# Gated linear attention and a feed-forward block on one core: scores computed over all 128 queries and masked 512 columns at a time, from the ninth chunk on

## The chip, the cores and the metric

The kernel runs on one NeuronCore of a Trainium2 chip. The metric is the device time of one execution in microseconds (us), given as the median of several runs. Beside the timed runs there is one profiled execution, from which all the views of the profile are read.

## What is computed

The reference has two stages. The first is a gated recurrence over 768 steps, for 4 batches and 8 heads of 48 values each. The second is a feed-forward block on the 3072 resulting rows of 384 values.

```python
for t in range(S):                                   # S = 768, D = 48
    state = alpha[:, :, t, :, None] * state + einsum('bhd,bhe->bhde', k[:, :, t], v[:, :, t])
    y[:, :, t] = einsum('bhd,bhde->bhe', q[:, :, t], state)
x = y.transpose(0, 2, 1, 3).reshape(B * S, H * D)    # 3072 x 384
a = x @ w1
b = x @ w2
out = ((a * b) @ w3) @ w_out
```

## The kernel before

The recurrence is done in chunks of 128 steps: 24 chunks (4 batches of 6), numbered n = 0 to 23, of all 8 heads at once. For a chunk, the products of the gates become a prefix sum of logarithms (`logs`, `decays`), its exponential scales k and q (`decayed`, DVE, L354), and 16 TensorE transposes with two ScalarE copies (`transposed`, L376 and L378) put k and q with their 48 values on the partitions (`qkT`). The heads stand in pairs: head 2j (called i = 0) on partitions 0 to 47, head 2j+1 (i = 1) on partitions 64 to 111, for j = 0 to 3. Then

- `scores(n)`: for each head, keys times queries, a 128 x 128 block. The blocks of the four heads of one i fill one bank of PSUM, `sc[i]`, of 512 columns. Scores of a key that is later than the query have to become zero, so VectorE writes `ms`, the scores and-ed bit by bit with a mask of all ones and zeros (L452, or L435).
- `attend_state(n-1)` (L469) brings in what earlier chunks left in the state; `attend(n-1)` (L477, L480) multiplies the values with the masked scores of the chunk before, and ScalarE copies the result out (L484).
- `outer(n)` (L388) and `advance(n)` carry the state on.

Up to chunk 7 a head's scores are one matmul over the whole width of the array (L449), and a mask is one instruction of 512 columns per i (L452). From chunk 8 on (`TURNED = 8`), `turned_scores` uses the array as four quarters of 64 x 64. The row half of a quarter is given by i, its column half by where the output lies: for i = 0, keys 0 to 63 (part 0) go to partitions 0 to 63 of the bank and keys 64 to 127 (part 1) to partitions 64 to 127; for i = 1 the two halves are exchanged ("turned"), so that the four matmuls of one j lie in four different quarters. Keys of part 1 are later than queries 0 to 63, so their matmul covers only the 64 queries 64 to 127; a part 0 matmul covers all 128. The 64 x 64 block that is left out is neither computed nor masked, and no one reads it: `attend_low` (L414) multiplies queries 0 to 63 with keys 0 to 63 alone, over half the rows of the array, and `attend` (L477) does queries 64 to 127 with all 128 keys. Two `attend_low` matmuls of the chunk before follow the four score matmuls of each j. For i = 1 the values, too, are needed with their halves exchanged: `turn_v` (GpSimd, L166) makes that copy.

Because of the block left out, the masks are four instructions per chunk (L435): for each i one of 64 partitions x 256 columns (queries 0 to 63; for i = 1 it begins at partition 64) and one of 128 x 256.

Beside the chunks, the same loop converts the weights of the feed-forward block from 64-bit words (`to_fp32`, L238 to L248, then L255 to L260), stores the attention's output to memory (L300), reads it back in groups of three chunks (`load_x`, L496), splits it into three parts (`split_x`, L502 on ScalarE, L503 and L504 on VectorE), and already runs `early_gate`, the products with w1 and w2 (L510), whose results ScalarE (L519) and VectorE (L521, L558) take out of PSUM. After the chunks come the rest of these products and the fold of w3 with w_out, and at last the product with the folded weights; all three run L510.

What sets the order: each engine works through its own queue in order[...]. The queue's order isn't that of the source; a scheduler lays it out when the program is built, by its own estimate of what each instruction takes, within the limits that the kernel gives with `tc.issue_after`. The same scheduler chooses for each of the 430 tiles taken with `bank()` one of the 8 banks of PSUM. A matmul that starts a tile waits until the tile that had this bank before has been read.

Of the kernel before, what the change touches and what calls it, by code (L numbers as in the profile page):

```python
# [12 lines left out]
I32 = mybir.dt.int32  # L13
# [3 lines left out]
ALU = mybir.AluOpType  # L17
# [31 lines left out]
def kernel(  # L49
# [12 lines left out]
    nc = tc.nc  # L62
    B, H, S, D = q.shape
    C = 128
# [4 lines left out]
    NP = H // 2  # L69
    DP = 64  # L70
# [34 lines left out]
    def bank():  # L105
        return ps.tile([C, 512], FP32, tag="bank", name="bank")
# [53 lines left out]
    def turned(n):  # L160
        return TURNED <= n < N
# [30 lines left out]
    keep = p1.tile([C, C], I32, name="keep")  # L192
    keep_turned = p1.tile([C, 2, DP], I32, name="keep_turned")
# [12 lines left out]
    keep_bc = keep[:, None, :].to_broadcast([C, NP, C])  # L206
    for half in range(2):
        nc.gpsimd.tensor_copy(out=keep_turned[ds(DP * half, DP), 1 - half], in_=keep[ds(DP * half, DP), ds(DP * half, DP)])
    nc.gpsimd.memset(keep_turned[DP:, 1], -1)
    for x in qks:  # L210
        nc.vector.memset(x[:, :, :, D:], 0.0)
    make_identity(nc, ident)
# [197 lines left out]
    def attend_low(n, jj, i, half):  # L410

        s, w = ds(DP * i, DP), (vts[n % 2] if i else st["v", n])
        h = half * NP // 2 + jj
        nc.tensor.matmul(st["y", n][0][i][ds(DP * half, DP), jj, 0:DP], w[s, h if i else 2 * h, :],  # L414
                         st["ms", n][s, i, h, 0:DP], start=(n % NCH == 0 and jj == 0), stop=True, skip_group_check=True)

    def turned_scores(n):

        qkT = st["qkT", n]
        sc = [bank().rearrange("p (j c) -> p j c", j=NP) for _ in range(2)]  # L420
        for j in range(NP):
            for part in range(2):
                for i in range(2):
                    r, t = ds(DP * i, D), slice(DP * part, C)
                    nc.tensor.matmul(sc[i][ds(DP * (part ^ i), DP), j, t], qkT[r, 0, j, ds(DP * part, DP)],  # L425
                                     qkT[r, 1, j, t], start=True, stop=True)
            if turned(n - 1):
                for i in range(2):
                    attend_low(n - 1, j % 2, i, i ^ (j < 2))
        ms = work.tile([C, 2, NP, C], FP32, tag="ms", name="ms")  # L430
        for i in range(2):
            r = ds(DP * i, DP)
            low, high = (keep_turned[r, 0], keep_turned[:, 1]) if i else (keep[r, 0:DP], keep[:, DP:])
            for x, mask, t in ((slice(DP * i, DP * (i + 1)), low, slice(0, DP)), (slice(0, C), high, slice(DP, C))):
                masked = nc.vector.tensor_tensor(ms[x, i, :, t].bitcast(I32), sc[i][x, :, t].bitcast(I32),  # L435
                                                 mask[:, None, :].to_broadcast([x.stop - x.start, NP, DP]),
                                                 op=ALU.bitwise_and)
        ends_of_part1[0] = mark["ms", n] = masked.ins
        st["ms", n] = ms

    def scores(n):
        if turned(n):
            return turned_scores(n)
        qkT = st["qkT", n]
        sc = [bank().rearrange("p (j c) -> p j c", j=NP) for _ in range(2)]
        for j in range(NP):
            for i in range(2):
                r = ds(DP * i, D)
                nc.tensor.matmul(sc[i][:, j, :], qkT[r, 0, j, :], qkT[r, 1, j, :], start=True, stop=True)  # L449
        ms = work.tile([C, 2, NP, C], FP32, tag="ms", name="ms")  # L450
        for i in range(2):
            masked = nc.vector.tensor_tensor(ms[:, i].bitcast(I32), sc[i].bitcast(I32), keep_bc, op=ALU.bitwise_and)  # L452
        ends_of_part1[0] = mark["ms", n] = masked.ins
        st["ms", n] = ms
# [345 lines left out]
    low, high = range(FH), range(FH, KF)  # L800
# [74 lines left out]
```

## Time and profile before

| | us |
|---|---|
| median of 3 runs | 471.29 |
| lowest and highest | 470.62, 471.86 |
| the profiled execution | 472.93 |
| its span in the trace | 471.20 |
| of the span: chunks 0 to 7, up to the first turned scores | 69.6 |
| of the span: turned chunks 8 to 23, and the last attend | 69.6 to 186 |
| of the span: rest of the feed-forward block | 186 to 471.2 |

The views of the profile give busy time by engine: PE is TensorE's matmuls, PEld its weight loads, DVE VectorE, ACT ScalarE, POOL GpSimd, SP the queue of most DMAs. An fp32 matmul appears as two records, one for each pass over its columns. The end of a matmul is modelled, so the distance from one start to the next says more than the length of a record. Every line of a list of waits names the instruction that waited, what it waited for, the total, the number of times and the longest.

### The profile page before, as it was taken

How to read it: one execution, taken by the hardware profiler on the slowest of the kernel's cores; microseconds unless marked ns; L12 is line 12 of the kernel's file. 1: busy time of each engine (PE TensorE's matmuls, PEld its weight loads, DVE VectorE, ACT ScalarE, POOL GpSimd, SP SyncE). 2: the span in 40 equal slices, each digit the busy share in tenths (PEclk: the TensorE clock that was granted, in tenths of full speed). 3: DMA queues.
4: the chain of work that ended last, by engine and by line, in shares of the span. 5: the costliest groups of instructions: out<-in, count | busy, mean ns of one | idle time of the engine just before them, and what ended most of it. 6: DMA issues, size and time to landing. Idle time of an engine off the chain costs nothing.

```text
span 471.2 us, 11168 instructions
## 1 busy us (share of the span) xinstructions
PE 453.1 (96%) x4360; PEld 430.4 (91%) x4360; DVE 363.5 (77%) x610; ACT 278.9 (59%) x552; POOL 96.0 (20%) x186
## 2 busy tenths in 40 slices
PE   4996999999999999999999999999999999999996
PEld 2675889898999989999999999999999999999996
DVE  2876997999979898999999968764542977766771
ACT  4864975767767554889787656554553633333330
POOL 6332243234313550222221111111011000000000
PEclk9999999999999999999999999999999999999999
DMA  9999999999999953566685433212013886555511
GB/s 182 251 189 247 239 226 207 222 218 207 203 207 209 266 141 116 170 185 220 205 297 190 133 124 101 85 50 85 35 51 111 245 243 184 176 160 167 173 52 50
DMA packets 145668, 80.36 MB, mean 171 GB/s; under 512 B 96240, under 2 KB 137456, under 8 KB 145616
## 3 DMA queue, kind: packets, MB, share of 16 engines
q1 hardware_dynamic: 139840, 64.44, 55.2%
q0 software_dynamic: 5776, 15.22, 10.3%
q8 instruction: 34, 0.56, 0.5%
q14 instruction: 18, 0.15, 0.1%
HBM read 57.58 MB, written 22.06 MB: 169 GB/s over the span
## 4 chain that ended last, share of the span: by engine, by line
PE 86%; DMA 5%; DVE 4%; ACT 3%; issue 1%; SPq 0%; DVEq 0%; ACTq 0%
PE bank L510 70%; DMA kq<-in_q_dram 3%; PE bank L425 3%; PE bank L376 2%; PE bank L477 2%; PE bank L469 2%; PE bank L612 1%; PE bank L388 1%; PE bank L338 1%; PE bank L341 1%; DMA raw<-in_moe_w_dram 1%; PE bank L480 1%; DVE qk L354 1%; PE bank L414 1%; PE bank L449 1%
## 5 line engine op out<-in xcount | busy, mean ns | idle before, releaser
L510 PE MATMUL bank<-x,w 128*128 128x384 f32 x1152 | 212.4, 338 | 1.9 <-DVE ms L435 0.9
L510 PEld LDWEIGHTS bank<-x,w 128*128 128x128 f32 x1152 | 199.9, 188 | 4.4 <-DVE ms L435 1.0
L510 PE MATMUL bank<-w3o,ab 128*128 128x384 f32 x576 | 100.2, 336 | 0.0
L510 PEld LDWEIGHTS bank<-w3o,ab 128*128 128x128 f32 x576 | 99.8, 188 | 0.0
L535 ACT ACTIVATE bank<-bank 128x384 f32<-128x384 f32 x96 | 45.6, 476 | 43.0 <-PE bank L510 42.8
L519 ACT ACTIVATE t<-bank 128x384 f32<-128x384 f32 x64 | 31.6, 495 | 54.8 <-PE bank L510 54.6
L585 POOL DMA_DIRECT2D abd<-ab x45 | 25.7, 570 | 143.4 <-DVE ab L571 126.8
L571 DVE TENSOR_TENSOR ab<-bank,r 128x384 f32<-128x384 f32 x44 | 24.4, 555 | 25.6 <-ACT bank L535 16.4
L378 ACT COPY qkT<-bank 128x512 f32<-128x512 f32 x48 | 26.0, 591 | 24.2 <-PE bank L376 24.2
L641 DVE TENSOR_TENSOR ab<-abl,ab 128x1024 fp32r<-128x1024 f32 x24 | 29.4, 1224 | 13.0 <-ACT ab L640 13.0
L640 ACT ACTIVATE ab<-abl 128x1024 fp32r<-128x1024 f32 x24 | 25.5, 1061 | 20.2 <-PE bank L510 18.0
L510 PE MATMUL bank<-wo,w3T 128*128 128x384 f32 x192 | 35.9, 334 | 0.0
L354 DVE TENSOR_TENSOR qk<-kq,e 128x768 f32<-128x768 f32 x24 | 23.3, 971 | 15.0 <-ACT e L345 7.5
L510 PEld LDWEIGHTS bank<-wo,w3T 128*128 128x128 f32 x192 | 33.5, 188 | 0.0
L243 ACT ACTIVATE power<-power,rebias 128x512 uint32<-128x512 uint32 (+1 forms) x36 | 25.1, 700 | 12.2 <-DVE power L242 12.1
L521 DVE SCALAR_TENSOR_TENSOR o<-bank,t 128x384 f32<-128x384 f32 x24 | 13.4, 557 | 22.4 <-issue 13.7
L642 DVE SCALAR_TENSOR_TENSOR ab<-ab,abl 128x1024 fp32r<-128x1024 f32 x24 | 29.2, 1219 | 0.0
L521 DVE SCALAR_TENSOR_TENSOR r<-bank,t 128x384 f32<-128x384 f32 x40 | 22.1, 552 | 6.8 <-ACT t L519 4.1
L245 DVE SCALAR_TENSOR_TENSOR mant<-mant,rest 128x512 f32<-128x512 uint32 (+1 forms) x36 | 23.6, 655 | 2.0 <-ACT rest L238 1.9
L238 ACT ACTIVATE rest<-raw 128x512 f32<-128x512 uint32 (+1 forms) x36 | 23.4, 652 | 1.0 <-DMA raw<-in_moe_w_dram 1.0
L166 POOL COPY vt<-v 64x192 f32<-64x192 f32 x32 | 19.4, 606 | 22.0 <-DMA v<-in_v_dram 21.0
L246 DVE SCALAR_TENSOR_TENSOR power<-raw,power 128x512 uint32<-128x512 uint32 (+1 forms) x36 | 23.3, 655 | 0.3 <-ACT power L243 0.2
(104 smaller groups left out, 685.9 us busy)
## 6 DMA issues: line engine op xcount, KB each, us to landing
raw<-in_moe_w_dram SPq DMA_DIRECT2D x28, 512.0 KB, 5.3
abl<-abd SPq DMA_DIRECT2D x24, 512.0 KB, 4.3
abd<-ab POOLq DMA_DIRECT2D x45, 192.0 KB, 3.1
xT<-xd POOLq DMA_DIRECT2D x9, 576.0 KB, 4.4
kq<-in_k_dram SPq DMA_DIRECT2D x24, 192.0 KB, 5.0
kq<-in_q_dram SPq DMA_DIRECT2D x24, 192.0 KB, 5.8
xd<-x SPq DMA_DIRECT2D x48, 96.0 KB, 3.9
out_dram<-o SPq DMA_DIRECT2D x24, 192.0 KB, 3.4
```

The source lines that it names most:

```text
L243: nc.scalar.activation(power, power, AF.Relu, scale=2.0 ** 23, bias=rebias)
L354: mark["qk", n] = nc.vector.tensor_mul(qks[n % 3][:, :, :, 0:D], st.pop(("kq", n)), st.pop(("e", n)).rearrange("p i (h d) -> p i h d", h=H ...
L378: mark["qkT", n] = nc.scalar.copy(qkT[:, :, :, ds(DP * half, DP)], tp[half]).ins
L510: nc.tensor.matmul(p, w[part][i], x[part][i], start=start and part == parts[0] and i == 0, stop=stop and part == parts[-1] and i == n - 1, ...
L519: nc.scalar.activation(t, p1, AF.Copy, scale=(1.0 + 1.0 / P) * scale)
L521: nc.vector.scalar_tensor_tensor(to, p2, scale, t, op0=ALU.mult, op1=ALU.add)
L535: nc.scalar.activation(p, p, AF.Copy, scale=1.0 + 1.0 / P)
L571: nc.vector.tensor_mul(ab, p, r[0])
L585: (nc.gpsimd if late else nc.sync).dma_start(out=abd[g][:, f, :], in_=ab)
L640: nc.scalar.activation(t[:, 0], ab, AF.Copy, scale=1.0 - 2.0 ** -13)
L641: nc.vector.tensor_sub(t[:, 1], ab, t[:, 0].bitcast(FP32))
L642: nc.vector.scalar_tensor_tensor(t[:, 2], t[:, 0].bitcast(FP32), -1.0 - 1.0 / P, ab, op0=ALU.mult, op1=ALU.add)
```

## The change

`turned_scores` now computes part 1, too, over all 128 queries; its 64 x 64 blocks that no one reads are computed and then masked to zero. That makes a mask one instruction of 128 partitions x 512 columns per i. For i = 1 the mask is the 128 x 128 tile `keep_turned`, read whole; its quarter that was never used (partitions 0 to 63, first 64 columns) is now set to 0 by one more memset in the setup. The `attend_low` matmuls stand in two groups of four, after j = 1 and after j = 3, one in each quarter of the array, instead of two after every j. The values stay in their two copies, and `attend`, `attend_low` and everything after the chunks are as they were. Line numbers in the text are those of the kernel before.

```diff
@@ setup
     nc.gpsimd.memset(keep_turned[DP:, 1], -1)
+    nc.gpsimd.memset(keep_turned[0:DP, 0], 0)
@@ turned_scores
         for j in range(NP):
             for part in range(2):
                 for i in range(2):
-                    r, t = ds(DP * i, D), slice(DP * part, C)
-                    nc.tensor.matmul(sc[i][ds(DP * (part ^ i), DP), j, t], qkT[r, 0, j, ds(DP * part, DP)],
-                                     qkT[r, 1, j, t], start=True, stop=True)
-            if turned(n - 1):
-                for i in range(2):
-                    attend_low(n - 1, j % 2, i, i ^ (j < 2))
+                    r = ds(DP * i, D)
+                    nc.tensor.matmul(sc[i][ds(DP * (part ^ i), DP), j, :], qkT[r, 0, j, ds(DP * part, DP)],
+                                     qkT[r, 1, j, :], start=True, stop=True)
+            if turned(n - 1) and j % 2:
+                for half in range(2):
+                    for i in range(2):
+                        attend_low(n - 1, j // 2, i, half)
         ms = work.tile([C, 2, NP, C], FP32, tag="ms", name="ms")
         for i in range(2):
-            r = ds(DP * i, DP)
-            low, high = (keep_turned[r, 0], keep_turned[:, 1]) if i else (keep[r, 0:DP], keep[:, DP:])
-            for x, mask, t in ((slice(DP * i, DP * (i + 1)), low, slice(0, DP)), (slice(0, C), high, slice(DP, C))):
-                masked = nc.vector.tensor_tensor(ms[x, i, :, t].bitcast(I32), sc[i][x, :, t].bitcast(I32),
-                                                 mask[:, None, :].to_broadcast([x.stop - x.start, NP, DP]),
-                                                 op=ALU.bitwise_and)
+            mask = keep_turned.rearrange("p x c -> p (x c)")[:, None, :].to_broadcast([C, NP, C]) if i else keep_bc
+            masked = nc.vector.tensor_tensor(ms[:, i].bitcast(I32), sc[i].bitcast(I32), mask, op=ALU.bitwise_and)
```

## The prediction

> **What bounds the kernel now.** I read first the busy times of the page, then the same by stretches of time, then who TensorE waited for while the turned chunks run, and last the order of time inside one score block.
>
> ```profile
> span 471.2 us, 11168 instructions
> PE 453.1 (96%) x4360; PEld 430.4 (91%) x4360; DVE 363.5 (77%) x610; ACT 278.9 (59%) x552; POOL 96.0 (20%) x186
> ```
>
> ```profile
> 68.00:92.00 24.00, 23.51 (x415) 21.50 (x417) 20.70 (x40) 16.44 (x38) 6.87 (x15) 1.00 0.94 208
> 92.00:116.00 24.00, 23.32 (x458) 21.17 (x451) 23.56 (x47) 16.36 (x37) 8.48 (x16) 1.00 0.98 215
> ...
> 186.00:300.00 114.00, 114.00 (x666) 113.87 (x667) 105.20 (x193) 88.21 (x176) 22.12 (x36) 1.00 0.53 173
> ```
>
> In the second fence the columns after the length are the busy times of PE, PEld, DVE, ACT and POOL. PE is the bound: over 23 of 24 us while these turned chunks run, all of the time from 186 to 300. DVE is close behind, 23.56 of 24 us from 92 to 116. So DVE's work matters only where PE waits for it:
>
> ```profile
> PE bank L510 <- DVE ms L435: 0.9, 2, 0.7
> PE bank L510 <- ACT qkT L378: 0.5, 1, 0.5
> PE bank L469 <- DVE ms L435: 0.3, 1, 0.3
> PE bank L425 <- ACT w L255: 0.2, 1, 0.2
> ```
>
> From 68 to 186 us the masks hold PE three times, for 1.2 us in all; these are matmuls that need a bank which the mask hasn't read yet. That is about what a faster mask can win directly. Now one score block, chunk 11:
>
> ```profile
> 91.32 0.67 PE L469 MATMUL bank<-qkT,T 48*64 48x128 f32 x16
> 91.81 0.38 PE L425 MATMUL bank<-qkT 48*64 48x128 f32 x7
> ...
> 92.80 0.22 PE L414 MATMUL bank<-ms,v 64*64 64x64 f32 x1
> ...
> 92.86 0.22 PE L414 MATMUL bank<-ms,v 64*64 64x64 f32 x1
> ...
> 93.03 0.71 PE L376 MATMUL bank<-ident,qk 64*128 64x64 f32 x16
> ```
>
> The block takes 1.22 us, from the first L425 to the first L376, and so in 11 of the 15 blocks with L414; the other four take 1.26.
>
> [...] the 16 passes of L469, 128 columns each over the four quarters, are through in 0.49 us (91.32 to 91.81), while on one quarter a pass follows the one before after 0.109 us. [...] at 172.5 (last fence) a copy stands behind an instruction that waits.
>
> **The change part by part.**
>
> *TensorE.* No instruction is added; per chunk the 8 part 1 matmuls grow from 64 to 128 columns. In the single starts of the trace a pass on one quarter takes 0.109 us for 128 columns and 0.058 for 64 (L414 above: 92.80, 92.86). Every matmul has two passes, and each quarter gets four score matmuls and two of L414. Before, the two quarters of part 0 had 4 x 2 x 0.109 + 2 x 2 x 0.058 = 1.10 us, the two of part 1 had 4 x 2 x 0.058 + 0.23 = 0.70. Afterwards all four have 1.10. The block lasts as long as its fullest quarter (1.10, and 0.12 until L376 begins, makes the 1.22 measured), so the added 0.40 us lies beside what the other two do: 0. The lower bound is -0.04 x 16 = -0.6 us, if the even grouping takes away the hiccup of the 1.26 blocks everywhere; the upper bound, no cover at all, is 16 x 0.40 = 6.4 us. I take 0, since L469 already shows four quarters at 128 columns each with no loss. Chunk 8, without L414, stays at 4 x 2 x 0.109.
>
> *VectorE.* Both shapes stand in the profile:
>
> ```profile
> L452 DVE TENSOR_TENSOR ms<-bank,keep 128x512 int32<-128x512 int32 x16 | 10.4, 683 | 0.0
> L435 DVE TENSOR_TENSOR ms<-bank,keep_turned 64x256 int32<-64x256 int32 x16 | 6.9, 428 | 0.5
> L435 DVE TENSOR_TENSOR ms<-bank,keep 128x256 int32<-128x256 int32 x16 | 6.5, 405 | 0.0
> ```
>
> Consecutive DVE instructions overlap, so I count from start to start. The four masks of a chunk take 0.334 + 0.437 + 0.442 + 0.342 = 1.555 us (chunk 11: starts at 95.39, 95.72, 96.16, 96.60 and the next instruction at 96.94)[...]. Two masks of 512 columns take 0.601 + 0.598 = 1.20 (chunks 0 to 7). DVE saves 0.355 us per chunk, 16 x 0.355 = 5.7 us. Since PE is the bound, nearly all of it becomes idle time of DVE. The memset in the setup, 0.15 us on POOL like its neighbour, lies between 1.8 and 3.7 us, when PE waits for the first gates: 0.
>
> *The order of the queues.* In the built programs PE's order is the same but for the L414. ACT, DVE, SP and POOL are laid out anew in places, and banks are assigned anew. Four places matter.
>
> 1. Chunk 6. Before, ACT puts one L484 copy (50.55) ahead of an L243 that waits for DVE until 51.80; now both copies stand behind it. The second, and all that follows, comes 0.25 us later. The third transposes after it need the first copy's bank, and the chain goes on to L502 and L273, for which PE stands still until 60.11: +0.25.
>
> 2. Chunk 11. PE waits 0.30 us at 96.0 for the first two masks, done at 96.13. Now an L239 and an L242 (0.33 + 0.34) stand ahead of the masks. Saved since 87 are 0.36 for chunk 10's masks and 0.06 on this one (0.68 instead of 0.74 until i = 0 is read): 0.67 - 0.36 - 0.06 = +0.25.
>
> 3. Chunk 13. L469 waits 0.45 us more than usual at 110.3 for the masks, the scores after it 0.39 for the last mask's bank (ended at 111.68; the profile names L255, which ends then too). Now the scores take a bank that was copied at 109.6, but the second half of L469 takes that of the turned mask, done at about 111.0 (masks begin 0.36 earlier and last 1.28). One stall of about 0.45 stays, the other goes: -0.3.
>
> 4. Chunk 22, the largest:
>
> ```profile
> 170.33 0.59 ACT L378 COPY qkT<-bank 128x512 f32<-128x512 f32 x1 [0.68 <-PE bank L376]
> 172.51 0.72 ACT L243 ACTIVATE power<-power,rebias 128x512 uint32<-128x512 uint32 x1 [1.60 <-DVE power L242]
> 173.15 0.56 ACT L378 COPY qkT<-bank 128x512 f32<-128x512 f32 x1
> ```
>
> One qkT copy stands ahead of L243, which waits for DVE, and one behind it. Now both stand behind. The bank of the first is the one for the L510 matmuls that start at 172.4; they wait until the copy ends, 173.15 + 0.56 = 173.71, and run 0.56 until 174.3. Before, the next group began at 173.80, after its own 0.88 us of waiting for a mask: +0.5.
>
> On SP the store of results, the loads of kq and the read-back L496 change places, but these loads run more than 10 us ahead (L496 issued at 150.54, used at 167.36): 0, and as much as they come late if that lead were used up.
>
> **The sum.** 0 + 0.25 + 0.25 - 0.3 + 0.5 = +0.7 us on the span of 471.2. The profiled execution itself took 472.93, 1.7 more than its span and 1.6 more than the median of the runs, so I carry the difference to the median: 471.29 + 0.7, forecast 472.0. About 0.3% (1.4 us) is what a measurement of this kernel can tell from no change; the forecast lies within it.
>
> **The rivals.**
>
> *The masks do win.* If the order moves cost nothing and all stalls that end with a mask go (0.30, 0.45, 0.39, 0.88), the time falls by 2.0 to 469.3. For it: three of them are named in the waits. Against: at 172 PE waits for L243 whatever the masks do, and all of PE's stalls from 68 to 186 are only some 3 us.
>
> *ACT's queue is the worse for it (slower).* The place is L243, which waits for DVE, ahead of copies that free banks. At chunk 22 its start follows L503, L504, L239 and L242 on DVE. If DVE reaches L242 there a microsecond later than at 172.5, PE stands still that microsecond more, since it has nothing else to run. Two such places with 0.8 us each and my +0.7 give 473.6. It decides from 0.7 us beyond what I reckoned. For it: the queues are laid out by estimates, and DVE's slow L242 (0.72 us in the record, 0.42 at most other places) beside two POOL copies shows that they needn't hold. Against: DVE has 0.73 us of idle time ahead of L503.
>
> *The columns aren't hidden.* If two quarters of the same rows share a limit that L469 doesn't show beside L414, the block grows by up to 0.40: 472.0 + 6.4 = 478.4.
>
> **How the numbers follow.** Forecast 66%, reaching from 470.3 to 472.7; masks win 7%; ACT's queue 21%, 472.7 to 474; columns not hidden 6%. The range goes from 470.3 to 474.0: it leaves out the unhidden columns, most of the win and a little of ACT's tail, about 15%. Faster by over 0.3% (below 469.9): 0.06. Slower (above 472.7): 0.21 + 0.06 = 0.27. Within: 0.67.
>
> **What would show it.** Score blocks from first L425 to first L376 still at 1.22; a block of 1.6 makes the third rival right. DVE's busy time about 5 to 7 us less (records, which overlap: for a chunk 1.665 now and 2 x 0.683 then, 16 x 0.30 = 4.8), the two masks 1.2 us from start to start. PE idle at 172.4 until about 173.7 on L378, and the first L510 of chunk 7 at about 60.4. If PE's stalls from 68 to 186 sum to under 1.5 us, my reckoning of the order is wrong; if PE stands still at places where it doesn't now, the second rival is at work.

## The result: 1.2% slower

| | before | after |
|---|---|---|
| median, us | 471.31 (6 runs) | 477.36 (6 runs) |
| ratio, 95% interval | | 1.012, 1.0086 to 1.0153 |
| the profiled execution, us | 472.93 | 477.86 |
| its span, us | 471.2 | 476.2 |
| of it, from the first score matmul of chunk 8 to the end, us | 401.7 | 408.2 |

The forecast of 472.0 and its range, up to 474.0, are both missed. Lines of the changed kernel stand one further than those of the kernel before up to the scores, and two earlier behind the masks: the wide scores are L426 (was L425), `attend_low` L415 (L414), the transposes L377 (L376), the qkT copies L379 (L378), the first feed-forward products L508 (L510). On POOL, `vt` stays L166, the decay products are L406 and L407 (L405, L406), the loads of the decays L363 (L362), the stores of end rows L327, L348 and L350 (L326, L347, L349).

### The profile page after: what moved, and what is told of

Read it like the earlier page. It is cut to its first block, busy times and chain, and to the rows that moved or that the text cites. A ratio compares the mean times of both kernels' runs of the same rounds, so it can differ in the third digit from the quotient of the medians.

```text
span 476.2 us, 11116 instructions
## 1 busy us (share of the span) xinstructions
PE 457.4 (96%) x4360; PEld 433.0 (91%) x4360; DVE 358.5 (75%) x578; ACT 279.1 (59%) x552; POOL 93.7 (20%) x187
## 4 chain that ended last, share of the span: by engine, by line
PE 81%; DMA 6%; DVE 6%; ACT 2%; issue 2%; SPq 1%; POOL 1%; POOLq 0%; DVEq 0%; ACTq 0%
PE bank L508 67%; PE bank L377 2%; PE bank L426 2%; DMA ac<-in_alpha_dram 2%; PE bank L467 2%; PE bank L475 1%; PE bank L610 1%; DMA dec<-ends 1%; DVE qk L355 1%; PE bank L389 1%; DMA kq<-in_q_dram 1%; PE bank L336 1%; DVE ms L450 1%; DMA xd<-x 1%; DMA raw<-in_moe_w_dram 1%
## 5 line engine op out<-in xcount | busy, mean ns | idle before, releaser
L508 PE MATMUL bank<-x,w 128*128 128x384 f32 x1152 | 213.5, 339 | 2.3 <-ACT qkT L379 1.7
L508 PEld LDWEIGHTS bank<-x,w 128*128 128x128 f32 x1152 | 200.7, 189 | 5.2 <-ACT qkT L379 2.3
L508 PE MATMUL bank<-w3o,ab 128*128 128x384 f32 x576 | 100.2, 336 | 0.0
L508 PEld LDWEIGHTS bank<-w3o,ab 128*128 128x128 f32 x576 | 99.9, 188 | 0.0
L379 ACT COPY qkT<-bank 128x512 f32<-128x512 f32 x48 | 25.9, 592 | 29.5 <-PE bank L377 29.5
L508 PE MATMUL bank<-wo,w3T 128*128 128x384 f32 x192 | 35.9, 334 | 0.0
L508 PEld LDWEIGHTS bank<-wo,w3T 128*128 128x128 f32 x192 | 33.5, 188 | 0.0
L244 ACT ACTIVATE power<-power,rebias 128x512 uint32<-128x512 uint32 (+1 forms) x36 | 25.1, 699 | 13.6 <-DVE power L243 13.4
L565 ACT ACTIVATE r<-bank 128x384 f32<-128x384 f32 x44 | 21.5, 489 | 1.6
```

Source lines behind the costliest of these rows:

```text
L244: nc.scalar.activation(power, power, AF.Relu, scale=2.0 ** 23, bias=rebias)
L379: mark["qkT", n] = nc.scalar.copy(qkT[:, :, :, ds(DP * half, DP)], tp[half]).ins
L508: nc.tensor.matmul(p, w[part][i], x[part][i], start=start and part == parts[0] and i == 0, stop=stop and part == parts[-1] and i == n - 1, ...
```

## The profile after

The head of the page, with the span and the busy times:

```profile
span 476.2 us, 11116 instructions
...
PE 457.4 (96%) x4360; PEld 433.0 (91%) x4360; DVE 358.5 (75%) x578; ACT 279.1 (59%) x552; POOL 93.7 (20%) x187
```

DVE is busy 5.0 us less than the 363.5 of before, with 32 instructions fewer: that is what the change set out to do. The groups of instructions by shape show the masks (busy us, mean ns of one, then idle time before them):

```profile
L435 DVE TENSOR_TENSOR ms<-bank,keep 128x512 int32<-128x512 int32 x16 | 10.9, 683 | 3.1 <-PE bank L426 3.0
L435 DVE TENSOR_TENSOR ms<-bank,keep_turned 128x512 int32<-128x512 int32 x16 | 10.9, 679 | 0.0
```

The score block of chunk 11, in the order of time, is as long as it was: from the first L426 to the first L377 it takes 91.52 - 90.30 = 1.22 us.

```profile
90.30 0.62 PE L426 MATMUL bank<-qkT 48*64 48x128 f32 x16
...
91.52 0.71 PE L377 MATMUL bank<-ident,qk 64*128 64x64 f32 x16
```

So both halves of the change do what they say. The list of what PE waited for between 68 and 186 us (total, times, longest) tells where the time went:

```profile
PE bank L415 <- POOL vt L166: 3.7, 1, 3.7
PE bank L508 <- ACT qkT L379: 1.7, 2, 1.1
PE bank L508 <- DVE ms L435: 0.2, 1, 0.2
```

The waits for masks have shrunk from 1.2 us to 0.2. But one wait is new: in the score block of chunk 14, PE stands still at an `attend_low` of chunk 13, which needs `vt`, the values with their halves exchanged. In the kernel before, the first such matmul of that block starts with no wait:

```profile
112.00 0.22 PE L414 MATMUL bank<-ms,vt 64*64 64x64 f32 x1
```

In the changed kernel, the order of time around it:

```profile
110.01 0.22 PE L415 MATMUL bank<-ms,v 64*64 64x64 f32 x1
113.96 0.37 PE L415 MATMUL bank<-ms,vt 64*64 64x64 f32 x1 [3.68 <-POOL vt L166]
```

The same stretch by windows, first in the kernel before, then in the changed one (the last three columns are the granted clock of TensorE, the DMA share and GB/s):

```profile
110.00:114.00 4.00, 3.47 (x94) 2.83 (x92) 3.96 (x8) 4.00 (x10) 0.68 (x1) 1.00 0.82 190
114.00:121.00 7.00, 7.00 (x100) 6.62 (x100) 6.38 (x13) 4.29 (x11) 4.03 (x8) 1.00 0.98 219
```

```profile
110.00:114.00 4.00, 0.32 (x16) 0.13 (x7) 2.78 (x3) 2.30 (x7) 1.47 (x5) 0.97 1.10 296
114.00:121.00 7.00, 7.00 (x87) 6.67 (x88) 3.71 (x6) 2.34 (x6) 2.40 (x6) 0.53 0.79 164
```

From one start to the next PE loses 3.9 us (3.7 of them idle), and then it works for 7 us at a granted clock of 0.53. By the trace's record of the clock TensorE ran at half for 6.83 us from 113.73 on (the mean from 113.72 to 120.56 is 0.50); in the kernel before, the clock is 1.00 on both stretches. Three more profiles with such a wait show the same in kind. In g4 (3.6 us of wait) the mean clock was 0.74 from 110 to 114 and 0.66 from 114 to 121, which makes some 6.8 us at half. In f1 (3.1 us) it was 0.76 from 114 to 121, and in g1 (3.7 us, at chunk 22) 0.77 from 171.6 to 179, which makes some 3.4 us in each. Why it is the one length or the other, these runs don't show. Measured by the starts of the score blocks, chunk 15 begins 6.9 us later against the kernel before than chunk 14 does: 3.9 for the wait and about 3 behind it, in the stretch at half clock.

Who held `vt` is seen on POOL. First the kernel before, POOL's instructions in the order of time (start, length, and in brackets the idle time before it and what ended it):

```profile
99.72 0.48 POOL L347 DMA_DIRECT2D ends<-e  x1 [1.34 <-ACT e L344]
102.41 0.49 POOL L326 DMA_DIRECT2D ends<-ac  x1 [2.20 <-DMA ac<-in_alpha_dram]
104.04 1.40 POOL L362 DMA_DIRECT2D dec<-ends  x2 [1.14 <-DMA ends<-e]
105.60 1.52 POOL L166 COPY vt<-v 64x192 f32<-64x192 f32 x2 [0.17 <-DMA v<-in_v_dram]
108.57 0.27 POOL L405 TENSOR_TENSOR dec<-dec 128x4 f32<-128x4 f32 x1 [1.44 <-DMA dec<-ends]
```

Then the changed kernel:

```profile
101.44 0.48 POOL L327 DMA_DIRECT2D ends<-ac  x1 [4.58 <-DMA ac<-in_alpha_dram]
101.92 0.48 POOL L348 DMA_DIRECT2D ends<-e  x1
105.33 1.40 POOL L363 DMA_DIRECT2D dec<-ends  x2 [2.93 <-DMA ends<-e]
112.35 0.49 POOL L406 TENSOR_TENSOR dec<-dec 128x4 f32<-128x4 f32 x1 [5.62 <-DMA dec<-ends]
...
113.18 0.73 POOL L166 COPY vt<-v 64x192 f32<-64x192 f32 x2
```

These rows are a round trip through memory. What a state decays by over chunk 14 is put together from three end rows of 384 values, which POOL stores to DRAM (`ends`) and loads back with the values on the partitions (`dec`); two small products (L406, L407) then make one factor of the three. Two pairs of chunk 14 have changed places:

- Move (a): the store of chunk 14's own row (L348) stood ahead of a store for chunk 16 (L327), which has to wait for the load of chunk 16's gates. Now it stands behind it and is issued 2.2 us later.
- Move (b): the copies `vt` of chunk 13 stood ahead of chunk 14's products. Now the products, which wait 5.62 us for the end of the round trip, stand ahead of the copies, which need nothing any more by then.

POOL works through its queue in order, as these rows show: the copies start at 113.18, behind products that waited until 112.35, though their values had landed by about 107 (SP issued that load at 100.01, and such loads took at most 6.3 us to land there). So PE waits for a transfer that it doesn't need yet. Chunk 22 has a move (b) as well; in this execution it costs nothing, since PE is 5 us late there already. Two more moves on POOL concern chunk 20's rows; the run g2 below leaves them as they are.

The rest is small. Chunk 8 begins 1.6 us earlier than in the kernel before, but that is chance: in the fourteen profiled executions of this case it begins between 66.9 and 70.0 us, with kernels of both kinds spread over that range. From here on, therefore, the profiles are also compared by the stretch from the first score matmul of chunk 8 to the end ("from chunk 8").

## The experiments

Theory: the loss is the order of POOL's queue, moves (a) and (b), and no part of it the wider scores or the masks. Rivals: the columns do cost; the masks or DVE's new order; SP's order, which changes from about chunk 17 on; and, within the theory, one move alone.

| label | kernel | median, us | ratio, 95% interval | from chunk 8, us | PE's wait for vt in the profile |
|---|---|---|---|---|---|
| f1_after_again | after, unaltered | 476.74 | 1.0099, 1.0076 to 1.0122 | 406.2 | 3.1, chunk 14 |
| e1_vt_first | after, (b) undone | 472.71 | 1.0029, 1.0011 to 1.0048 | 406.5 | 3.0, chunk 22 |
| e3_ends_direct | after, no wait for the gates on POOL | 472.13 | 1.0015, 0.9996 to 1.0033 | 406.4 | 3.7, chunk 22 |
| e4_four_masks_vt | as e1, four masks | 473.14 | 1.0032, 1.0017 to 1.0048 | 403.3 | none |
| f2_pool_order | after, POOL's order of before | 471.39 | 0.9995, 0.9984 to 1.0005 | 401.9 | none |
| f3_sp_order | after, SP's order of before | 476.99 | 1.0097, 1.0072 to 1.0122 | 407.9 | 4.1, chunk 14 |
| f4_both_orders | after, both | 472.37 | 1.0018, 1.0001 to 1.0034 | 402.0 | none |
| g1_e_first | after, (a) undone | 476.35 | 1.0105, 1.0073 to 1.0136 | 405.9 | 3.7, chunk 22 |
| g2_vt_e_first | after, (a) and (b) undone | 472.16 | 1.0018, 1.0003 to 1.0034 | 401.9 | none |
| e2_dec_first | before with (b) | 471.33 | 1.0002, 0.9988 to 1.0015 | 401.8 | none |
| g3_before_a | before with (a) | 471.63 | 1.0002, 0.9984 to 1.0020 | 401.5 | none |
| g4_before_ab | before with (a) and (b) | 477.03 | 1.0124, 1.0096 to 1.0151 | 407.0 | 3.6, chunk 14 |

The kernel before, run beside these, had medians of 471.52 (e), 471.54 (f) and 471.69 (g); the ratios are against these.

### One move, in each kernel

In the changed kernel the vt copies go ahead of the products again; nothing else in any queue moves but at chunks 14 and 22 of POOL's:

```diff
-                nc.gpsimd.tensor_copy(out=vts[n % 2][ds(DP * half, DP), :, 0:D],
-                                      in_=st["v", n][ds(DP * (1 - half), DP), 1::2, 0:D])
+                mark["vt", n] = nc.gpsimd.tensor_copy(out=vts[n % 2][ds(DP * half, DP), :, 0:D],
+                                                      in_=st["v", n][ds(DP * (1 - half), DP), 1::2, 0:D]).ins
@@ advance(n)
-        nc.gpsimd.tensor_mul(dec, d[:, 0, :], d[:, 1, :])
+        with after_marks(*[("vt", n - 1)] * turned(n - 1)):
+            nc.gpsimd.tensor_mul(dec, d[:, 0, :], d[:, 1, :])
```

> The changed kernel with one line of order: POOL must issue the two vt copies of chunk n-1 before the decay products of chunk n. Only POOL's queue differs from the changed kernel's, at chunks 14 and 22; the matmuls, the masks and the other queues are the same. Theory A (the loss is POOL's queue at chunk 14): PE's 3.7 us wait at attend_low of chunk 13 and the half clock of 6.8 us behind it go, together about 7 us at that place; the time falls from 477.4 to between 470 and 471.5. Rival B (the wider score columns, or the other moves of the queues, cost the time, and PE would lose it elsewhere): the time stays at 476 to 478. Rival C (the decay rows come late for PE anyway, and the wait only moves to chunk 14's own use of them): 473 to 475.

472.71, with single executions from 470.98 to 477.23. Most of the loss goes, but not all, which none of the three theories had said. The profiled execution, the slowest of the 22, shows no wait at chunk 14 but one at chunk 22. POOL's rows there:

```profile
167.24 1.39 POOL L363 DMA_DIRECT2D dec<-ends  x2 [4.09 <-issue]
168.68 2.79 POOL L166 COPY vt<-v 64x192 f32<-64x192 f32 x2
```

Here it is no longer the products but the decay loads of chunk 22 that stand ahead of the copies of chunk 21. They fetch what the store before them has to bring to memory first, and they go some 4.6 us later than in the kernel before (L362 at 162.64 there). The profile names no releaser for this wait of 4.09 us; in e3 the same loads wait for the landing of the store. Besides, the two copies take 2.79 us here, where those of chunk 13 took 1.36 in this run and 0.73 in the changed kernel: 1.4 to 2.1 of the 3.0 us that PE waits. So POOL's chain of round trips and PE's chain run side by side, and the copies can be caught behind the first at several places.

In the kernel before, move (b) alone, at chunk 14:

```diff
+    def decay_rows(n):
+        if n in ends and ("dec", n) not in st:
+            dec, d = work.tile([C, NP], FP32, tag="dec", name="dec"), decs[n // 2 % 2]
+            nc.gpsimd.tensor_mul(dec, d[:, 0, :], d[:, 1, :])
+            mark["dec", n] = nc.gpsimd.tensor_mul(dec, dec, d[:, 2, :]).ins
+            st["dec", n] = dec
@@ the loop over n
-        turn_v(n)
+        if n + 1 in (14,):
+            decay_rows(n + 1)
+        with after_marks(*[("dec", n + 1)] * (n + 1 in (14,))):
+            turn_v(n)
```

> The kernel before with only POOL's queue changed, at one place: the two decay products of chunk 14 stand ahead of the two vt copies of chunk 13. Nothing of the score columns or masks changes. Theory A: the products wait for the decay loads, which landed at about 108.5 in the kernel before, so the vt copies end at about 110.8 instead of 107.2, and attend_low of chunk 13, which starts at 111.3 there, is held by 0 to 4 us, more if the loads land later, plus up to 3 us of half clock: 471.5 to 478, and PE waits for vt at that place. Rival B (the order of POOL is harmless and the loss is in the columns): 471.3, no wait for vt.

471.33: no loss, and no wait for vt. That is what rival B had said, and theory A's range (471.5 to 478) just misses it: the products alone, put ahead of the copies, don't make the loss. This run can't tell whether the columns do, since it has none of them. The decay loads were in at 107.2, the copies were over at 108.9, and PE used them first at 109.63: 0.8 us to spare. Move (b) by itself is harmless as long as the round trip is early.

The changed kernel without POOL's wait for the gates of chunk 16, by a store that reads them from DRAM:

```diff
-            nc.gpsimd.dma_start(out=ends[n][2:3], in_=a[0:1])
+            b, c = divmod(n, NCH)
+            nc.gpsimd.dma_start(out=ends[n][2:3].rearrange("m (h d) -> m h d", h=H), in_=alpha[b:b + 1, :, c * C, :])
```

> The changed kernel, but the third row of the chunk ends is loaded from the decays in DRAM directly, instead of from the tile that another load has to fill first. So POOL's queue doesn't wait for that load (4.6 us at 101.4), and the round trip through DRAM can begin earlier; the decay products still stand ahead of the vt copies. Theory A (what holds the products is the length of the chain load, ends, store, load): the decay loads of chunk 14 land up to 4 us earlier, PE's 3.7 us wait shrinks to 0 to 1 us and the half clock goes: 470 to 473. Rival B (the columns cost): 476 to 478. Rival C (the round trip is bound by DMA traffic, not by the load ahead of it): the decay loads land within 1 us of 112.2 and the time stays above 475.

472.13, as theory A had it. The decay loads of chunk 14 are in at 107.4 instead of 112.4; rival C falls. Again the profiled execution has its wait at chunk 22 instead.

As the first, but with the four old masks (narrow ones, which leave the unread blocks alone) on the wide scores:

```diff
-            mask = keep_turned.rearrange("p x c -> p (x c)")[:, None, :].to_broadcast([C, NP, C]) if i else keep_bc
-            masked = nc.vector.tensor_tensor(ms[:, i].bitcast(I32), sc[i].bitcast(I32), mask, op=ALU.bitwise_and)
+            r = ds(DP * i, DP)
+            low, high = (keep_turned[r, 0], keep_turned[:, 1]) if i else (keep[r, 0:DP], keep[:, DP:])
+            for x, mask, t in ((slice(DP * i, DP * (i + 1)), low, slice(0, DP)), (slice(0, C), high, slice(DP, C))):
+                masked = nc.vector.tensor_tensor(ms[x, i, :, t].bitcast(I32), sc[i][x, :, t].bitcast(I32),
+                                                 mask[:, None, :].to_broadcast([x.stop - x.start, NP, DP]),
+                                                 op=ALU.bitwise_and)
```

> The changed kernel with the vt copies ahead (as in the first run) and the four old masks in place of the two whole ones: the widened score matmuls alone. Theory A (columns hidden, the masks worth about nothing): within 0.7 us of the first run, 470 to 472; DVE's busy time back to about 363.5. Rival B (the whole masks are what wins): 1.5 to 2.5 us above the first run. Rival C (columns cost): 476 or more, score blocks above 1.25 us.

473.14, 0.4 above the first, with intervals that overlap: what the whole masks are worth can't be told from nothing. One sign speaks for the masks: in this profile they hold PE for 1.3 us from 66 to 190 (0.2 in the profiles of the first experiment and of f2), and the stretch from chunk 8 takes 403.3 us, 1.3 to 1.8 more than in the six other profiles without a wait for vt. It is one execution. POOL, SP and ACT are laid out here just as in the first experiment; it is the change of the matmuls (wider scores, `attend_low` in fours), not that of the masks, that the scheduler answered with a new order.

### Whole queues

> The changed kernel once more, unaltered, in more executions and beside the variants below, to see how fixed its loss is. Theory A (POOL's queue at chunk 14 holds the vt copies behind the decay products every time): 476 to 478.5 in nearly all executions, PE waits some 3 to 4 us for vt in chunk 14's score block. Rival (the wait hangs on how the transfers happen to land): the times spread from 471 to 478, as those of the variant with the copies ahead did (471.0 to 477.2).

476.74, between 474.70 and 477.74: the loss is in every execution, though its size differs by up to 3 us between them.

For the next three, each DMA of SP and each instruction of POOL is held behind the one that precedes it in the list of the kernel before (`QUEUES`, one name per place in the source), as far as the order of the source lets it. Shown is POOL's part:

```diff
+QUEUES = {
+    'POOL': 'g1 g1 g1 g1 g2 g2 ...',
+}
...
+    def put(site, call, *args, **kw):
...
+        ahead = [x for x in done_here if x[0] < rank]
+        with ExitStack() as stack:
+            if ahead:
+                stack.enter_context(tc.issue_after(max(ahead, key=lambda x: x[0])[1]))
+            r = call(*args, **kw)
+        done_here.append((rank, r.ins))
+        return r
...
-        nc.gpsimd.tensor_mul(dec, d[:, 0, :], d[:, 1, :])
+        put("g19", nc.gpsimd.tensor_mul, dec, d[:, 0, :], d[:, 1, :])
```

> The changed kernel with POOL's queue put back into the order of the kernel before (from chunk 8 on all but one place the same: the decay loads of chunk 20 stay ahead of the vt copies of chunk 19); score matmuls, masks and SP's order are the changed kernel's. Theory A (POOL's order alone is the loss): 470.5 to 472, no wait for vt at chunk 14; the decay loads of chunk 14 land at about 108.5 instead of 112.2. Theory A2 (POOL and SP together: a wait for vt at chunk 22 stays because SP issues the loads of the decays later and weight loads earlier): 471.5 to 473.5 with a spread of some 5 us. Rival B (columns, masks or DVE's order): 475 or more.

> The changed kernel with SP's queue alone put back into the order of the kernel before (stores, the loads of kq and of the output weights, from about chunk 17 on); POOL's order stays the changed kernel's. Theory A (POOL): the wait for vt at chunk 14 comes before any of SP's moves and stays, 475.5 to 478. Rival (SP's order is the loss): 470.5 to 472.

> The changed kernel with POOL's and SP's queues both in the order of the kernel before (but for that one place on POOL and one on SP); ACT's queue then stands as before too but for one pair. What is left of the change is the wider score matmuls, the whole masks and DVE's new order. Theory A (the loss is the order of POOL and SP): 470 to 471.5, the spread of the kernel before (470.3 to 475.5, most below 472). Rival B (the columns or DVE's order cost something by themselves): 472.5 or more. My own sum for DVE's and PE's part was -0.5 to +0.7.

With POOL's order put back the whole loss is gone: 471.39, ratio 0.9995, 5.3 us under the unaltered kernel of the same chip. PE no longer waits for vt; what it waits for most from 68 to 186 us is a copy on ACT (calls through `put` carry a line of it, 129):

```profile
PE bank L538 <- ACT qkT L129: 2.2, 2, 1.1
```

SP's order alone does nothing (476.99 beside 476.74). In f2's trace the other queues are nearly the changed kernel's: ACT's two moves at chunk 6 and one mask on DVE went back with POOL's order, and on SP three transfers changed places after 130 us. So this also gives the worth of the rest of the change, the wide scores, the whole masks and the new orders of DVE and SP and of ACT at chunk 22 together: 0.9984 to 1.0005 of the time before, or -0.75 to +0.24 us. The columns rival is out. With both orders put back the time was 472.37, 1 us above POOL's alone, above what theory A gave it and just under what rival B did; its profile shows no wait for vt, and why it is a little slower stays open.

### Both moves, and each alone

Move (a) undone in the changed kernel, at its one place:

```diff
-            mark["pool"] = nc.gpsimd.dma_start(out=ends[n][0:1], in_=e[0:1, 0]).ins
+            mark["pool"] = mark["e0", n] = nc.gpsimd.dma_start(out=ends[n][0:1], in_=e[0:1, 0]).ins
@@ logs(n)
-            nc.gpsimd.dma_start(out=ends[n][2:3], in_=a[0:1])
+            with after_marks(*[("e0", 14)] * (n == 16)):
+                nc.gpsimd.dma_start(out=ends[n][2:3], in_=a[0:1])
```

> The changed kernel with one pair on POOL put back: the store of chunk 14's end row (ends<-e) goes ahead of the store ends<-ac of chunk 16, which waits for a load; the decay products stay ahead of the vt copies. Every other queue and place is the changed kernel's. Theory A (two moves on POOL have to come together: the store held behind a wait, and the copies behind the products): the store goes 2 to 3 us earlier, the decay loads land at 107 to 109.5, the products let the copies through at about 109 to 110.5, and PE, which needs them at 110, waits 0 to 1 us: 471 to 473.5. Rival (the place of the products alone is the cause): 475 to 478, PE waits 3 us or more at chunk 14.

The mechanism at chunk 14 came as theory A said; the time is the rival's. The store goes at 99.44, the decay loads land at 108.4, the copies end at 110.3, and the block of chunk 14 takes 1.37 us: nothing is left of the wait there. But the time is 476.35, as before. PE's waits, and below them POOL at chunk 22:

```profile
PE bank L416 <- POOL vt L166: 3.7, 1, 3.7
```

```profile
165.25 1.40 POOL L364 DMA_DIRECT2D dec<-ends  x2 [4.93 <-issue]
168.57 0.74 POOL L407 TENSOR_TENSOR dec<-dec 128x4 f32<-128x4 f32 x1 [1.91 <-DMA dec<-ends]
169.38 1.19 POOL L408 TENSOR_TENSOR dec<-dec,dec 128x4 f32<-128x4 f32 x1
170.64 2.04 POOL L166 COPY vt<-v 64x192 f32<-64x192 f32 x4
```

The same stall has moved to the second move (b): products of chunk 22 ahead of the copies of chunk 21, which PE needs at 167.7 and gets at 171.6. In the unaltered kernel the first stall covers the second, for PE comes there 5 us later and POOL doesn't. Undoing one of two stalls in a row uncovers the other.

Both moves undone (this edit and that of the first experiment):

> Both moves of POOL's queue at chunk 14 put back (the store ahead, and the vt copies ahead of the products there and at chunk 22); SP, ACT, DVE, PE and the rest of POOL as in the changed kernel. Theory A: 470.8 to 472.3, like the kernel with POOL's whole order put back (471.4), since the store that goes earlier takes the later decay chains with it and the wait at chunk 22 that the first variant showed goes. Rival (the rest of POOL's order at chunks 16 to 22 matters too): as the first variant, 472 to 473.5 with a spread of 6 us.

472.16, within theory A's numbers, and no wait for vt in the profile. Here the queues of SP, ACT and DVE stand in the trace exactly as in the changed kernel, and POOL's differs at these places alone. Most executions lie between 470.9 and 472.7, four of 22 at 474.4 to 475.7; but the kernel before, too, has five of 43 at 474.6 to 477.4 in these runs, so such times aren't the change's own. The interval still excludes 1, where that of POOL's whole order doesn't: 0.1 to 1.6 us remain, and where they go stays open.

Now the other way round: the kernel before, with its narrow scores and four masks. Move (a) alone: chunk 14's store and its decay loads are issued after the store of chunk 16's gates.

```diff
         if n in ends:
-            mark["pool"] = nc.gpsimd.dma_start(out=ends[n][0:1], in_=e[0:1, 0]).ins
+            def send():
+                mark["pool"] = nc.gpsimd.dma_start(out=ends[n][0:1], in_=e[0:1, 0]).ins
+                load_ends(n)
+            if n == 14:
+                held.append(send)
+                return
+            send()
...
-        load_ends(n)
@@ the loop over n, after logs(n + 4)
+            if n == 12:
+                with after_marks(("ac", 16)):
+                    held.pop()()
```

> The kernel before, and on POOL alone, at one place, the store of chunk 14's end row behind the store ends<-ac of chunk 16, which waits for a load. The vt copies of chunk 13 stay ahead of the decay products. Theory A (the moves have to come together): the decay loads land 2 to 3 us later, at about 111, but only the state product of chunk 14 waits for them, which PE needs from about 120 on: 471 to 472. Rival: 474 or more.

471.63: no loss, although the decay loads now land at 111.1. The copies don't stand behind the products that wait for them:

```profile
107.41 0.96 POOL L166 COPY vt<-v 64x192 f32<-64x192 f32 x2
111.11 0.19 POOL L412 TENSOR_TENSOR dec<-dec 128x4 f32<-128x4 f32 x1 [2.73 <-DMA dec<-ends]
```

And both moves, this edit with `decay_rows(14)` from above:

> The kernel before with both of POOL's moves at chunk 14 made (the store behind the wait, the decay products ahead of the vt copies), everything else as before: narrow score matmuls and four masks. Theory A: the loss of the change comes back without the change: the store at about 101.5, the decay loads land some 10 us later (7.7 to 12.6 in the runs so far), at about 111.5, the copies end at 113, PE waits 2 to 4 us at about 110.5 and runs at half clock afterwards: 474 to 477.5. Rival (the loss needs the wider columns or DVE's new order): 471 to 472.5.

477.03, ratio 1.0124: the loss of the change, 1.012, without the change. PE's waits and POOL's rows:

```profile
PE bank L427 <- POOL vt L166: 3.6, 1, 3.6
```

```profile
100.57 0.49 POOL L326 DMA_DIRECT2D ends<-ac  x1 [3.50 <-DMA ac<-in_alpha_dram]
101.05 0.49 POOL L350 DMA_DIRECT2D ends<-e  x1
...
111.56 0.61 POOL L410 TENSOR_TENSOR dec<-dec 128x4 f32<-128x4 f32 x1 [4.68 <-DMA dec<-ends]
...
112.69 0.73 POOL L166 COPY vt<-v 64x192 f32<-64x192 f32 x2
```

It is the picture of the changed kernel, within a microsecond: store at 101.05 (101.92 there), products at 111.56 (112.35), copies at 112.69 (113.18), and PE 3.6 us late (3.7). SP, ACT and DVE keep the order of the kernel before in this trace. In that kernel neither move costs anything alone, and both together cost 5.3 us. Together with g2, which takes the moves out of the changed kernel and all but 0.1 to 1.6 us of the loss with them, this shows the cause.

No run beat the kernel before by more than its interval.

## Why the prediction was wrong

*TensorE, 0: right.* Twelve blocks of the changed kernel take 1.22, two 1.27, and the one of chunk 14 is the stall (1.37 in f2, g1 and g2, where the stall is gone). The upper bound of 6.4 us came close to the time lost, and the third rival, "the columns aren't hidden", to the time measured (478.4), by a mechanism that isn't there.

*VectorE, 5 us of busy time that are worth about nothing: right.* 363.5 to 358.5; the two masks of chunk 11 start at 93.98 and 94.59, and the next instruction at 95.18, 1.20 us as reckoned. The waits for masks did shrink by 1 us, but the rest of the change with POOL's order put back gains 0.15 us, with an interval that holds 0.

*The order of the queues: here it failed.* The text said that "ACT, DVE, SP and POOL are laid out anew in places" and went on "Four places matter"; of POOL's places none was followed to what waits on it. That step put the wait of PE for `vt` at nothing without a reason. What it needed stood in the trace of before and in the order of the two programs: the copies of chunk 13 ended at 107.1 and PE wanted them from about 112 on. Behind the products, which began at 108.57, they would have ended at about 110 (0.74 for the products, 0.73 for the copies), 2 us early. But move (a) takes 3.2 us of that: the store would go not at 99.72 but once L326 is issued, at 102.9. That is a microsecond too late, by an estimate from one execution, on a trip of which the runs show 7.8 to 12.6 us from the store to the products. So this working would have found the place, and a wait of about 1 us with a long tail; it would not have given the size, nor the half clock behind the wait. The term stood at 0 in the sum, for it wasn't there; it measured 6.9 us at chunk 14 in the profile and 5 to 6 us on the time.

*The four places that were priced.* Three had the wrong sign: chunk 6 gave -0.29 where +0.25 was reckoned (PE's gap at L508 is 0.35 us over its usual spacing, 0.64 before), chunk 11 -0.04 for +0.25, chunk 13 -0.76 for -0.3, chunk 22 about -0.1 for +0.5. At chunk 22 the wait stood where it was said to, on the copy behind L244 (L243 before), 1.2 us long; but the kernel before lost 0.4 and 0.9 us at that place, and the two together are as much. Between chunks 19 and 20 PE lost about 0.6 us that the text hadn't named (two gaps at 155.7 and 157.0). These are differences of a few tenths between two single executions and none of them decides.

*SP, 0: right* (476.99 with SP's old order, 476.74 without).

*The rivals.* The slower one, "ACT's queue", had the right kind of mechanism, an instruction that waits standing ahead of one that PE needs, and the reason for it too: the queues are laid out by estimates that needn't hold. Its sign, PE standing still where it didn't before, came true. But it looked on ACT; the waits of before, from 68 to 186 us, name ACT and DVE and not POOL. A queue that no wait names has only never been late yet.

## What to carry to other kernels

When a change makes a scheduler lay out the queues anew, follow every pair that changes places on every engine, the idle ones too: ask whether the one that is now ahead waits for something far away (a trip through memory), and how much room the one behind it had. Two moves that are harmless alone can share one margin, so price them together. And look for a second stall of the same kind further on: while the first one stands, the second is covered, and undoing the first alone gains nothing (476.35 beside 476.74).

## What the runs showed that was not expected

- A wait of 3.9 us on PE cost 6.9: the clock then stood at half for 6.83 us. In the unaltered kernel's second profile, with a wait of 3.1 us, the mean clock from 114 to 121 was 0.76, which makes some 3.4 us at half, and the stretch from chunk 8 to the end was 2 us shorter.
- From POOL's store of a row of 384 values to the first use of what is loaded back took 7.8 us in one execution (f2, 99.19 to 106.95) and 12.6 in another (f3, 101.16 to 113.79), in the same program but for the order of queues.
- The first 68 us of the kernel vary by 3 us from execution to execution (chunk 8 begins between 66.9 and 70.0), more than most of what was priced in the prediction; the stretch after it repeats within 0.5 us (401.5 to 402.0 in six of the seven profiles without a wait for vt; 403.3 in the seventh, which has four masks on the wide scores).
